# Token order, masked band products on TensorE, double weight pieces and paired inner tiles in a fused attention and gated-MLP kernel

## The chip, the cores and the metric

One core of one Trainium2 chip runs the whole program. TensorE (PE) does the products, VectorE (DVE) and ScalarE (ACT) the element work, GpSimd (POOL) some element work and some transfers, SyncE (SP) issues most transfers. The metric is the device time of one execution in microseconds, the median of several runs. The profile comes from one further execution.

## The reference, cut to what matters

```python
def attention(q, k, v):                  # 8 batches, 8 heads, 576 tokens, 64 wide
    q_d, k_d, v_d = (mean over each 4 tokens of q, k, v)         # 144 tokens
    out_d = softmax(q_d @ k_d.T / 8) @ v_d                       # "coarse"
    out_local = softmax(q @ k.T / 8 where |i - j| < 4) @ v       # "band"
    return repeat(out_d, 4) + out_local

x = attention(q, k, v) as (4608 tokens, 512)
xn = x / sqrt(mean(x * x) + 1e-6) * rms_g
out = (silu(xn @ w_gate) * (xn @ w_val)) @ w_out                 # inner width 1536
```

The weights reach the chip as 64-bit floats, 18.9 MB in all; everything else is 32-bit.

## The kernel before

**Tokens and chunks.** The 4608 tokens are worked in 18 chunks (`NCH`) of 256. A chunk is two units of 128 tokens. A unit takes tokens from both batches of a pair of batches, a stretch of four (`US`) out of each of 16 segments per batch, so all coarse output of two batches must stand before the first chunk of that pair.

**Coarse attention.** A coarse unit (class `Coarse`) is one batch and one pair of heads, 32 in all: scores on PE (L499), peaks on DVE (L508, L513), exponents on ACT (L518), turns on PE (L527), copies on ACT (L534), values on PE (L541), the share on DVE (L547, L550, L554). The result is written to DRAM and read back in token order (`load_up`), and DVE adds it (L846). The sums over four tokens come, for the first two batches, from PE products with the identity (class `OpeningSums`, L408) and DVE additions (L429), and for later ones from adding transfers that POOL issues (L362).

**Band attention.** Class `Attention` has, per chunk, four times two products of q with shifted k on DVE (L758, 128x896) and their sums (L762), a softmax over seven neighbours, products of the shares with shifted v (L812 on DVE, L805 on ACT), and the sum over neighbours: on DVE (L831), in chunks 0 and 1 on PE (L827, products with the identity). Then the root of the mean square (L863 to L886), the norm (L895), turns on PE (L907), and a split of x into a high and a low part (L911 on ACT, L915 on DVE), since products are made of two reduced-precision parts.

**The MLP.** For each of 12 inner tiles `f` PE does 12 gate and 12 value products of 128x256 (L976), ACT the tanh (L983), DVE the gate and the product (L986, L991, 128x256 each), ACT the high part (L997), DVE the low part (L1000), and PE six second products of 128x512 (L1011), two tiles later (`LAG` = 2). Gate and value of a tile share one PSUM bank. ACT evicts the result (L1018).

**The weights** are decoded in 36 pieces of 128x512: fetch the raw 64 bits (L250), scale on ACT (L254), gather the last bits on POOL (L264), join on DVE (L271), high part on ACT (L281, L283), low part (the split) on DVE (L295 with the gain, L293) or, for `w_out`, on whichever of DVE and POOL the planner picks. The scaled copy stands in a tile of its own.

```python
        def decode(n):                                   # before, shortened
            at = due[0] - 16 + 1.4 * n
            ...
            join_ = task("DVE", 0.78, join, at, [scaled, bits], uses=[raw, w])
            hi = task("ACT", 0.7, high, at, [join_, *own], uses=[w])
            if n in gained:
                whole[n] = task("DVE", 0.85, lambda: split("dve"), at, [hi], uses=[w])
```

**What sets the order.** For the opening, chunks 0 to 2 and the attention of chunk 3, class `Plan` sorts tasks like the ones above: each has an engine, a written cost, a due time, what it comes after and the buffers it takes; the planner walks a model clock and, on each engine, emits the ready task with the earliest due time. From chunk 3 on a loop emits in written order, with the attention and two coarse units for the next chunk laid between the inner tiles, and a scheduler places the instructions:

```python
        for f in range(NF):                              # before, from chunk 3
            fwd.emit(f)
            late.append((fwd, f))
            if len(late) > LAG:
                fw, g = late.pop(0)
                fw.emit_second(g)
            while todo and todo[0][0] < f + 1:
                todo.pop(0)[1]()
```

Thirty idle products on PE (L1105), fed by a copy on ACT (L1102), are planned from about 5 us with the latest due time of all.

## Time and profile before

| | us |
|---|---|
| runs | 1143.12, 1146.85, 1143.39; median 1143.39 |
| span of the profiled execution | 1142.6 |
| busy: PE, DVE, ACT, POOL | 1080.1, 963.1, 625.7, 173.0 |
| first gate product (L976) | 107.8 |
| end of chunk 0, 1, 2 (eviction L1018) | 186.3, 255.5, 316.3 |
| end of chunk 3, 4, 5 | 370.9, 444.1, 501.2 |
| end of the last chunk | 1138.3 to the last product, 1142.6 with its store |

How to read it: the time of the median run stands 0.8 us above the span, which is what lies around it. A chunk's length is the distance between the ends of two chunks. Busy shares are means over stages with different limits, so each stage is read by itself.

### The profile page before, as it was taken

To read this page: it belongs to the slowest core of one execution; us is meant where nothing else is said; L and a number is where in the kernel's file an instruction comes from. 1 tells how busy PE (TensorE), PEld (TensorE's weight loads), DVE (VectorE), ACT (ScalarE), POOL (GpSimd) and SP (SyncE) were. 2 spreads that over 40 slices of the span, in tenths; PEclk is the share of its full clock that TensorE was granted. 3 is DMA by queue.
4 is the path that set the end of the run, shared out by engine and by line. 5 is a ranking of instruction groups with operands and counts; after the bars stand their busy time and mean duration, and the time that the engine had idled before them with its cause. 6 is when DMAs were issued, how large, how long until landed. Compare 5 with 4: busy or idle time off the path is not lost.

```text
span 1142.6 us, 21949 instructions
## 1 busy us (share of the span) xinstructions
PE 1080.1 (95%) x8002; PEld 987.1 (86%) x8002; DVE 963.1 (84%) x1869; ACT 625.7 (55%) x2284; POOL 173.0 (15%) x205
## 2 busy tenths in 40 slices
PE   6883799999999999999999999999999999999998
PEld 4772688878898899999999999998999999999997
DVE  6786998788999989797989797979898989997432
ACT  1564663847383847474747474747465573838221
POOL 1654662334200010101010101000000000000000
PEclk8875999999999899999999999999999999999999
DMA  9986482446544443535253535222231313220000
GB/s 267 300 274 173 107 222 84 96 95 148 124 100 105 110 104 88 115 88 115 83 120 88 114 88 114 78 63 76 65 89 54 99 52 99 67 60 20 1 19 20
DMA packets 76813, 119.57 MB, mean 105 GB/s; under 512 B 26784, under 2 KB 36256, under 8 KB 76704
## 3 DMA queue, kind: packets, MB, share of 16 engines
q1 hardware_dynamic: 47520, 97.34, 28.8%
q0 software_dynamic: 8640, 15.93, 9.1%
q10 hardware_dynamic: 20544, 4.89, 2.0%
q8 instruction: 63, 1.03, 0.4%
q14 instruction: 46, 0.38, 0.1%
HBM read 106.33 MB, written 11.80 MB: 103 GB/s over the span
## 4 chain that ended last, share of the span: by engine, by line
PE 78%; DVE 8%; DMA 7%; ACT 2%; issue 2%; POOL 1%; SPq 0%; ACTq 0%; DVEq 0%; POOLq 0%
PE ps_h L976 48%; PE ps_o L1011 24%; PE ps_a L541 2%; PE ps_a L499 2%; DMA wg<-in_v_sum_dram 1%; DMA wg<-in_w_gate_dram 1%; DVE o_sb L271 1%; PE ps_a L907 1%; DMA qk<-in_qk_sum_dram 1%; DMA kv<-in_k_pad_dram 1%; DVE prod L812 1%; PE ps_a L527 1%; DVE prod L758 1%; ACT up_t L856 1%; ACT prod L805 1%
## 5 line engine op out<-in xcount | busy, mean ns | idle before, releaser
L1011 PE MATMUL ps_o<-wo,hs 128*128 128x512 f32 x1296 | 355.7, 399 | 5.4 <-POOL hs L1000 5.3
L976 PE MATMUL ps_h<-xh,wg 128*128 128x256 f32 x1728 | 349.1, 282 | 4.0 <-DVE wg L295 1.7
L976 PE MATMUL ps_h<-xh,wv 128*128 128x256 f32 x1728 | 341.8, 280 | 5.0 <-DVE sil L986 4.9
L976 PEld LDWEIGHTS ps_h<-xh,wg 128*128 128x128 f32 x1728 | 284.0, 190 | 13.0 <-ACT xh L911 2.2
L976 PEld LDWEIGHTS ps_h<-xh,wv 128*128 128x128 f32 x1728 | 280.5, 188 | 11.0 <-DVE sil L986 6.9
L805 ACT ACTIVATE prod<-kv,sc 128x64 f32<-128x64 f32 x1072 | 279.2, 405 | 18.1 <-DVE x_t L831 9.8
L1011 PEld LDWEIGHTS ps_o<-wo,hs 128*128 128x128 f32 x1296 | 221.2, 188 | 43.1 <-POOL hs L1000 8.4
L976 PE MATMUL ps_h<-xl,wg 128*128 128x256 f32 x864 | 243.5, 282 | 0.1
L976 PE MATMUL ps_h<-xl,wv 128*128 128x256 f32 x864 | 241.8, 280 | 0.0
L983 ACT ACTIVATE sil<-ps_h 128x256 f32<-128x256 f32 x216 | 82.4, 382 | 227.8 <-PE ps_h L976 216.0
L986 DVE SCALAR_TENSOR_TENSOR sil<-sil,ps_h 128x256 f32<-128x256 f32 x216 | 91.1, 422 | 94.9 <-ACT sil L983 83.5
L976 PEld LDWEIGHTS ps_h<-xl,wg 128*128 128x128 f32 x864 | 164.0, 190 | 6.9 <-DVE sil L986 1.3
L976 PEld LDWEIGHTS ps_h<-xl,wv 128*128 128x128 f32 x864 | 163.0, 189 | 1.6
L997 ACT ACTIVATE hs<-sil 128x256 fp32r<-128x256 f32 x216 | 89.3, 415 | 133.9 <-DVE sil L991 112.3
L758 DVE TENSOR_TENSOR prod<-q_t,kv 128x896 f32<-128x896 f32 x140 | 153.1, 1094 | 5.7 <-DMA q_t<-in_q_band_dram 5.4
L762 DVE TENSOR_REDUCE sc<-prod 128x14 f32<-128x896 f32 x144 | 155.3, 1085 | 0.4
L831 DVE TENSOR_REDUCE x_t<-prod 128x128 f32<-128x896 f32 x128 | 135.7, 1080 | 11.5 <-PE ps_a L907 4.5
L812 DVE TENSOR_TENSOR prod<-sc,kv 128x384 f32<-128x384 f32 (+2 forms) x144 | 119.6, 868 | 0.2
L1000 DVE TENSOR_TENSOR hs<-sil,hs 128x256 fp32r<-128x256 f32 x196 | 87.3, 447 | 23.3 <-ACT hs L997 23.2
L991 DVE SCALAR_TENSOR_TENSOR sil<-sil,ps_h 128x256 f32<-128x256 f32 x216 | 91.2, 422 | 6.4 <-PE ps_h L976 4.8
L362 POOL DMA_DIRECT2D qk<-in_qk_sum_dram x36 | 32.2, 894 | 319.6 <-DMA qk<-in_qk_sum_dram 275.1
L856 ACT ACTIVATE up_t<-x_t 128x128 f32<-128x128 f32 x144 | 44.2, 307 | 21.3 <-DVE x_t L846 12.7
(118 smaller groups left out, 974.7 us busy)
## 6 DMA issues: line engine op xcount, KB each, us to landing
kv<-in_k_pad_dram SPq DMA_DIRECT2D x72, 320.0 KB
kv<-in_v_pad_dram SPq DMA_DIRECT2D x72, 320.0 KB
qk<-in_qk_sum_dram POOLq DMA_DIRECT2D x36, 288.0 KB, 5.0
out_dram<-o_sb SPq DMA_DIRECT2D x36, 256.0 KB
q_t<-in_q_band_dram SPq DMA_DIRECT2D x70, 128.0 KB
vs<-in_v_sum_dram POOLq DMA_DIRECT2D x36, 144.0 KB, 3.6
...
```

Source lines behind the costliest of these rows:

```text
L758: nc.vector.tensor_tensor(out=pr, in0=bcast(q[:, s0:s0 + 2], 2, NO), in1=window(k, s0), op=ALU.mult)
L762: nc.vector.tensor_reduce(out=self.sc[:, j, par, s0:s0 + 2], in_=self.pr[i], axis=AX.X, op=ALU.add,)
L805: nc.scalar.activation(out=self.pr[i][:, o, s], in_=self.v[j, par][:, s0 + s + o], func=AF.Copy, scale=p[:, s, o:o + 1],)
L812: (nc.vector if engine == "DVE" else nc.gpsimd).tensor_tensor(out=self.pr[i][:, a:b], in0=bcast(p[:, :, a:b].rearrange("p s o -> p o s"), ...
L831: nc.vector.tensor_reduce(out=self.x[j][:, s0:s0 + 2, par], in_=pr.rearrange("p o s d -> p s d o"), axis=AX.X, op=ALU.add,)
L976: nc.tensor.matmul(out=self.p[f][:, t], lhsT=wi(f)[:, 0, k], rhs=xi[:, k], start=(n == 0), stop=(n == 3 * KT - 1),)
L983: nc.scalar.activation(out=self.sil[f], in_=self.p[f][:, 0], func=AF.Tanh, scale=0.5)
L986: nc.vector.scalar_tensor_tensor(out=self.sil[f], in0=self.sil[f], scalar=1.0, in1=self.p[f][:, 0], op0=ALU.add, op1=ALU.mult,)
L991: nc.vector.scalar_tensor_tensor(out=self.sil[f], in0=self.sil[f], scalar=0.5, in1=self.p[f][:, 1], op0=ALU.mult, op1=ALU.mult,)
L997: nc.scalar.activation(out=self.hs[f][:, 0], in_=self.sil[f], func=AF.Copy)
L1000: (nc.gpsimd if engine == "POOL" else nc.vector).tensor_tensor(out=self.hs[f][:, 1], in0=self.sil[f], in1=self.hs[f][:, 0], op=ALU.subtract,)
L1011: nc.tensor.matmul(out=self.o[j], lhsT=lhs[:, cols], rhs=rhs(f)[:, 0], start=(f == 0 and i == 0), stop=(f == NF - 1 and i == 2),)
```

## The change

1. *Tokens in order.* A unit is 32 consecutive groups of four tokens, for all heads. Batch b's four coarse units are needed only when its tokens come. Four coarse units stand in the opening, eight are planned during chunks 0 to 2, and the loop lays two per chunk from chunk 3. Loads of q, k, v and stores of the output are cut where batches and runs of nine groups end.
2. *Band attention of chunks 0 and 1 on PE* (class `Early`): scores of 128 tokens against their neighbourhood of 136, with a mask that a bf16 product adds (L1048, L1050), peaks on DVE (L1063), exponents on ACT (L1074), shares on DVE (L1101), turns (L1108, L1118) and value products (L1133) on PE. The coarse output is added by a product with a spread matrix (L1139) from SBUF, without the way through DRAM. The mask and the spread matrix are made on POOL at the start.
3. *Opening sums* for batch 0 alone, by a DVE sum over four raw slabs (L406) and, for v, additions on POOL and DVE (L415).
4. *No idle products.*
5. *Weights in double pieces*, 16 of 128x1024 and four of 128x512, decoded in place in the raw tile; the split always on DVE (L285 with the gain, L283).
6. *Inner tiles in pairs*: gate of two tiles, value of two tiles, and tanh, gate, product, high and low part once on 128x512 (L1266, L1269, L1274, L1283); second products (L1296) one pair later; gate and value in banks of their own; two buffers each for `sil` and `hs`.

```diff
-LAG = 2
-W_BUFS = 4
+LAG = 1
+W_BUFS = 2
 FIRST = 3
-EARLY = 7
-COARSE = {3: 1}
+ON_TENSOR = 2
...
-    spots = [f"first{n % 8}" for n in range(24)]
+    spots = [("first0", "first1", "first2", "first3", "second0", "second1")[n % 6] for n in range(12)]
+    spots += ["second0", "second1", "second0", "second1", "xh1", "xl1", "o_sb", "o_sb"]
...
-        join_ = task("DVE", 0.78, join, at, [scaled, bits], uses=[raw, w])
+        join_ = task("DVE", (0.78, 1.3)[m - 1], join, at, [scaled, bits], uses=[raw])
...
+        low = task("DVE", (0.75, 1.35)[m - 1], split, at, [hi], uses=[raw])
...
+    class Early:
+        def load_values(self, u):
...
+            for h in range(H):
...
+                nc.sync.dma_start(out=self.ve[u][h * EDGE:(h + 1) * EDGE, h * D:(h + 1) * D], in_=src)
+        def score(self, u, n):
...
+            nc.tensor.matmul(out=s, lhsT=one_sb, rhs=bcast(near_sb[:, FAC * (1 - lo):FAC * (1 - lo + NEAR_K)], 1, 2), start=True, stop=False)
+            for h in range(2):
+                nc.tensor.matmul(
+                    out=s[:, h].rearrange("p (n j) -> p n j", j=FAC), lhsT=q[:, h, FAC * n0:FAC * (n0 + GRP)],
+                    rhs=k[:, h, n0 - lo:n0 - lo + NEAR_K], start=False, stop=(h == 1),
+                )
...
-            n = min(COARSE.get(c, 2), len(coarse) - done)
+            n = min(2, len(coarse) - done)
...
-        for f in range(NF):
-            fwd.emit(f)
-            late.append((fwd, f))
...
+        for n in range(NF // 2):
+            for half in range(2):
+                (fwd.emit_value if half else fwd.emit_gate)(n)
+                if half:
+                    late.append((fwd, n))
+                    if len(late) > LAG:
+                        fw, g = late.pop(0)
+                        fw.emit_second(g)
+                while todo and todo[0][0] < 2 * n + half + 1:
+                    todo.pop(0)[1]()
```

**PE at the start.** In the rows below, `ps_a`, `ps_h` and `ps_o` are PSUM banks, `wo` and `wv` hold raw sums in the weights' later places, `qk` the sums, `near_sb` and `one_sb` the mask. Before:

```order
L1105 MATMUL ps_o<-hs 128x256 x21
L408 MATMUL ps_a<-wo_0_113,ident_sb 128x288 x8
L1105 MATMUL ps_o<-hs 128x256 x5
L408 MATMUL ps_h<-wo_0_138,ident_sb 128x288 x8
L499 MATMUL ps_a<-qk 72x144 x4
L408 MATMUL ps_a<-wv_0_171,ident_sb 128x288 x4
L499 MATMUL ps_h<-qk 72x144 x4
L527 MATMUL ps_a<-ident_sb,a_g 72x72 x8
```

And after the change, where `hs` is q in token order and `w_1_102` the raw k:

```order
L1048 LDWEIGHTS one_sb
L1048 MATMUL ps_h<-near_sb,one_sb 128x272
L1050 MATMUL ps_h<-w_1_102,hs 128x136 x2
L1048 LDWEIGHTS one_sb
L1048 MATMUL ps_h<-near_sb,one_sb 128x272
L1050 MATMUL ps_h<-w_1_102,hs 128x136 x2
L498 MATMUL ps_a<-qk 72x144 x4
L526 MATMUL ps_a<-ident_sb,a_g 72x72 x8
```

Sums and idle products are gone from the head of PE's row, and band scores stand there, ahead of the coarse scores.

**DVE around the first gate product.** The last thing that chunk 0's gate waits for is the low part of x, `xl`. Before:

```order
L295 SCALAR_TENSOR_TENSOR wg_0_409<-o_sb,g_sb,wg_0_408 128x4x128
L295 SCALAR_TENSOR_TENSOR wv_0_416<-o_sb,g_sb,wv_0_415 128x4x128
L915 TENSOR_TENSOR xl<-ps_a,xh 128x4x128 x2
L758 TENSOR_TENSOR prod<-q_t,kv 128x896
L762 TENSOR_REDUCE sc<-prod 128x14
L986 SCALAR_TENSOR_TENSOR sil<-sil,ps_h 128x256
```

After, where `wo_1_134` holds shares of the band attention and `w_2_216`, `w_2_281` raw pieces of weights:

```order
L1093 TENSOR_TENSOR prod<-wo_1_134,z_e 128x64
L1101 TENSOR_TENSOR wo_1_134<-wo_1_134,z_e 128x4x128 x2
L1063 TENSOR_REDUCE m_e<-ps_h 128x2
L1183 TENSOR_TENSOR xl_630<-ps_a,xh_629 128x4x128 x2
L1063 TENSOR_REDUCE m_e<-ps_h 128x2
L1067 TENSOR_SCALAR m_e<-m_e 128x4
L271 SCALAR_TENSOR_TENSOR w_2_216<-w_2_216 128x1024 x2
L271 SCALAR_TENSOR_TENSOR w_2_281<-w_2_281 128x1024
```

The low part moves from place 123 in DVE's row to place 78 (repeats counted once), and what stands ahead of it is now shares and peaks where band products, sums and splits stood.

**DVE within a later chunk.** Before:

```order
L812 TENSOR_TENSOR prod<-sc,kv 128x3x128
L986 SCALAR_TENSOR_TENSOR sil<-sil,ps_h 128x256
L885 TENSOR_TENSOR newton<-newton,rms 128x8
L812 TENSOR_TENSOR prod<-sc,kv 128x3x128
L991 SCALAR_TENSOR_TENSOR sil<-sil,ps_h 128x256
L886 SCALAR_TENSOR_TENSOR rinv<-newton,rinv 128x8
L895 TENSOR_TENSOR x_t<-x_t,rinv 128x512 x2
L1000 TENSOR_TENSOR hs<-sil,hs 128x256
```

After:

```order
L1269 SCALAR_TENSOR_TENSOR sil<-sil,ps_h 128x512
L1274 SCALAR_TENSOR_TENSOR sil<-sil,ps_h 128x512
L1283 TENSOR_TENSOR hs<-sil,hs 128x512
L874 TENSOR_REDUCE x_t<-prod 128x2x64 x2
L1269 SCALAR_TENSOR_TENSOR sil<-sil,ps_h 128x512
L934 TENSOR_TENSOR xl_8074<-ps_a,xh_8073 128x4x128 x2
L864 TENSOR_TENSOR prod<-sc,kv 128x3x128 x2
L1274 SCALAR_TENSOR_TENSOR sil<-sil,ps_h 128x512
```

Each pass of the inner tiles now covers two tiles, and band passes stand between a pair's gate and product as they stood between a tile's.

**SP ahead of the first weight.** After the change SP's row begins with the raw sums, four loads of v and 32 edge loads of 8x64, and only then come the weights:

```order
L1028 DMA wo_1_189<-in_v_pad_dram 128x8x64
L1036 DMA kv<-in_v_pad_dram 8x1x64 x8
L249 DMA w_2_216<-in_w_gate_dram 128x1024
L249 DMA w_2_216<-in_w_val_dram 128x1024
```

Before, eight loads of k and q, eight of raw sums and four of v stood there.

917 lines of the change are left out of this document (582 added, 335 removed).

## The prediction

> **What bounds the kernel now.** I read the slices of the span, then windows cut at the ends of chunks (the evictions of the second products, L1018), then the waits, the chain and the DVE groups of the opening. Columns of the windows: length, then busy time (instructions) of PE, PEld, DVE, ACT, POOL, then granted clock, DMA share, GB/s.
>
> ```profile
> PE   6883799999999999999999999999999999999998
> DVE  6786998788999989797989797979898989997432
> ...
> 0.00:107.80 107.80, 69.84 (x472) 57.60 (x472) 81.99 (x135) 49.26 (x156) 52.01 (x52) 0.78 0.88 264
> 107.80:186.30 78.50, 68.61 (x483) 62.11 (x484) 70.37 (x116) 47.37 (x118) 39.86 (x40) 0.97 0.55 138
> 186.30:255.50 69.20, 64.21 (x498) 56.44 (x497) 55.57 (x103) 38.92 (x150) 22.59 (x37) 1.00 0.41 97
> 255.50:316.30 60.80, 58.78 (x451) 53.16 (x450) 54.19 (x105) 33.16 (x129) 22.27 (x35) 1.00 0.60 132
> ...
> 370.90:444.10 73.20, 69.90 (x521) 64.32 (x522) 67.42 (x131) 49.88 (x200) 5.18 (x6) 0.95 0.38 93
> 444.10:501.20 57.10, 57.10 (x437) 52.27 (x435) 51.16 (x105) 33.39 (x130) 5.15 (x6) 1.00 0.43 102
> 842.60:893.40 50.80, 50.80 (x372) 47.71 (x371) 47.85 (x94) 28.78 (x110) 0.00 (x0) 1.00 0.27 76
> 1094.40:1142.60 48.20, 43.93 (x312) 40.64 (x311) 13.09 (x32) 9.99 (x24) 0.00 (x0) 1.00 0.06 23
> ```
>
> Two regimes. From about 444 us PE is busy for 57.10 of 57.10 us in a chunk that carries two coarse units and 50.80 of 50.80 in one that carries none, so one coarse unit costs (57.1 − 50.8)/2 = 3.15 us of PE, and nothing off PE counts there. The first 107.8 us hold no gate product; PE is busy 65% of them with sums, coarse units, turns and idle products, DVE 76%. Chunks 0 and 1 then take 78.5 and 69.2 us. What a chunk needs of PE follows from the dense stretches:
>
> ```profile
> 1131.46 2.75 PE ps_h L976 x24
> 1134.21 3.90 PE ps_o L1011 x17
> ```
>
> 114.6 ns for a gate or value product, 229 ns for a second product; 288 × 0.1146 + 72 × 0.229 = 49.5 us, some 50.5 with the turns of x (50.8 measured). So chunk 0 lost over 15 us beyond its other turns (112 of L827), and chunk 1 with some 3.6 coarse units (11 us) lost 69.2 − 50.5 − 11 = 7. What stood in the opening:
>
> ```profile
> PE ps_a L863 <- ACT up_t L856: 14.3, 1, 14.3
> PE ps_a L408 <- DMA wo<-in_qk_sum_dram: 5.0, 1, 5.0
> ...
> 8.39 15.59 DMA wg<-in_v_sum_dram
> 28.75 15.49 DMA wg<-in_w_gate_dram
> ...
> 87.32 3.94 DMA up<-o_g
> 92.28 4.22 DMA up_t<-up
> ...
> PE ps_h L976 <- DVE sil L986: 3.4, 2, 2.4
> PE ps_h L976 <- DVE wg L295: 1.7, 1, 1.7
> ```
>
> The first two are PE's waits before 107.8 (total, times, longest): coarse output written to DRAM and read back, 14.3 us at the end of the opening. The next four are from the chain (start, length). The last two are waits within chunk 0: the weights are decoded barely ahead of use.
>
> **The change, part by part.** The prices of DVE in the opening (count | busy, mean ns | idle before it):
>
> ```profile
> L762 DVE TENSOR_REDUCE sc<-prod 128x14 f32<-128x896 f32 x13 | 14.1, 1081 | 0.3
> L758 DVE TENSOR_TENSOR prod<-q_t,kv 128x896 f32<-128x896 f32 x9 | 10.2, 1132 | 5.4 <-DMA q_t<-in_q_band_dram 5.4
> L812 DVE TENSOR_TENSOR prod<-sc,kv 128x512 f32<-128x512 f32 x8 | 7.8, 980 | 0.0
> L271 DVE SCALAR_TENSOR_TENSOR o_sb<-o_sb,wg 128x512 uint32<-128x512 uint32 x8 | 5.4, 681 | 3.0 <-POOL wg L264 3.0
> L295 DVE SCALAR_TENSOR_TENSOR wg<-o_sb,g_sb,wg 128x512 fp32r<-128x512 f32 x5 | 4.5, 897 | 0.0
> L513 DVE TENSOR_SCALAR m_g<-m_g 72x4 f32<-72x4 f32 x8 | 3.8, 473 | 0.2
> L508 DVE TENSOR_REDUCE m_g<-ps_a 72x2 f32<-72x288 f32 x8 | 3.2, 443 | 0.0
> L554 DVE TENSOR_TENSOR o_g<-ps_a,z_g 72x256 f32<-72x256 f32 x4 | 1.6, 412 | 0.0
> L550 DVE RECIPROCAL z_g<-z_g 72x4 f32<-72x4 f32 x8 | 1.4, 174 | 0.3
> L429 DVE TENSOR_TENSOR vs<-vs,wg 72x512 f32<-72x512 f32 x2 | 1.4, 690 | 0.1
> ```
>
> From 512 to 896 elements per lane a pass grows from 0.69 to 1.08 us, 1.02 ns an element: I estimate 1.21 us for 1024 and 2.5 for the 2304 that one opening sum reads.
>
> *Opening, first gate product 107.8 → 70.* Leaving it: band products, sums and values of two chunks on DVE, four coarse units of eight, the idle products, PE's sums, the DRAM round trip. Ahead of chunk 0's last low part DVE's order now holds 2 opening sums (5.0), 14 peaks at about 0.43 (6.0), 4 coarse units at 2 × 0.44 + 2 × 0.47 + 0.17 + 0.41 = 2.4 (9.6), 6 double joins (7.3), 4 gained splits and 2 plain ones at 1.21 to 1.8 (8.3), 6 passes of shares (4.1), 6 copies, adds and lows (4.1) and some thirty small ones at 0.17 to 0.47 (6): 50 us where 82 stood. DVE was busy 80% from its first instruction, at about 5 us, to 107.8; the same share gives 62 us, and the sums must land first, about 7.5: 70. Lower bound 60: DVE never waits after the sums, 7.5 + 50, or the sixth weight piece paces it. SP now issues 32 small edge loads and 4 of values before the first weight, at 0.4 to 0.6 us each:
>
> ```profile
> 3.32 0.54 SPq L568 DMA_DIRECT2D kv<-in_k_pad_dram  x1
> ...
> 21.60 7.10 SPq L568 DMA_DIRECT2D kv<-in_v_pad_dram  x4
> 28.75 0.59 SPq L250 DMA_DIRECT2D wg<-in_w_gate_dram  x1
> ```
>
> 36 × 0.54 = 19 us put the first weight at about 24 us instead of 28.75; six pieces of 1.05 MB at 264 GB/s take 24 more, so the last lands near 50, and with its decoding and the rest of the row the gate opens past 60. Upper bound 82: DVE at 67% (waits on SP's loads, on POOL's thirteen steps of masks, on a slower PE). If each small load took 7.10/4 = 1.8 us, the first weight would come at 70 and nothing would be gained; those four queued behind large transfers, the small ones only behind two, so I stay near 0.54.
>
> *Chunk 0, 78.5 → 80.* It still waits for weights. From the first gate product to the last split of gate and value weights DVE's order holds 10 double joins and 4 single ones (14.9), 8 gained splits at 1.45 and 2 plain ones at 1.25, all of them now on DVE (14.1), peaks, shares and norm of chunk 1 (7.4), ten passes of the inner tiles (6.9) and six band products with their sums, for chunk 2 (13): 56 us, at chunk 0's share (70.37 of 78.5, 90%) 62.5. Behind the last split come four inner tiles' products (96 × 0.1146 = 11) and the second ones trailing (6): 80. Bounds 73 (share 1) and 90 (76%, DVE's share of the opening). PE's own work, less the 112 turns (L827), is not the limit here.
>
> *Chunks 1 and 2, 69.2 → 65 and 60.8 → 61.* PE content: 50.5 and four coarse units each, 63; DVE some 55 us at 0.9. Together the end of chunk 2 moves by −37.8 + 1.5 − 4.2 + 0.2 = −40.3.
>
> *Coarse units moved later: +9.4.* Batch order needs four at the start instead of eight, so 20 remain after chunk 2, where 17 stood: 3 × 3.15, on a full PE.
>
> *The seam in chunk 4: −3.* The window 370.90:444.10 holds 352 gate and value products, 72 second ones and about 2.5 units, 40.3 + 16.5 + 8 + 2 = 67 us of PE, so some 6.5 were lost; half, as DVE's inner-tile work falls. Bounds 0 and −6.5.
>
> *Pairs of inner tiles: 0.* PE's products stay 128x256 and 128x512 and as many. DVE's passes go from 36 to 18 per chunk at
>
> ```profile
> L986 DVE SCALAR_TENSOR_TENSOR sil<-sil,ps_h 128x256 f32<-128x256 f32 x216 | 91.1, 422 | 94.9 <-ACT sil L983 83.5
> ```
>
> 36 × 0.42 = 15.2 against 18 × 0.69 = 12.4, which is 2.8 us a chunk off an engine that has 6 free. Cover: after the values of pair p PE has the 48 products of pair p+1 (5.5 us) before it needs p's low part, and product, high, low take 0.69 + 0.59 + 0.69 = 2.0 with the eviction below for the high part; 3.5 us are left for queueing on DVE, where a band pass ahead takes 0.7 to 1.1.
>
> ```profile
> L1018 ACT COPY o_sb<-ps_o x2: 586/586/587, 185.7 to 186.4; 128x512 f32<-128x512 f32 x2
> 1138.14 1.07 ACT L1018 COPY o_sb<-ps_o 128x512 f32<-128x512 f32 x2 [2.08 <-PE ps_o L1011]
> ```
>
> *Loads and stores in pieces.* Nothing in the middle: chunk windows show DMA at 0.27 to 0.43, and SP issues up to a chunk ahead. The last store goes in some five issues instead of one, 4 × 0.54 less overlap: +0.7, bounds 0 and 2.
>
> Sum: −40.3 + 9.4 − 3 + 0.7 = −33.2 against the profiled span of 1142.6: 1109.4. The median of the runs, 1143.39, is 0.8 above that span: 1110.
>
> **A rule weighed.** The clock as rows show it:
>
> ```profile
> 28.00:57.00 29.00, 25.39 (x186) 21.02 (x185) 22.79 (x42) 16.00 (x56) 17.53 (x17) 0.88 0.98 298
> 86.00:114.00 28.00, 9.16 (x49) 7.85 (x48) 19.35 (x36) 12.18 (x33) 13.08 (x12) 0.54 0.59 174
> ```
>
> With PE 88% busy 0.88 was granted, and 0.54 in the stretch that holds the wait of 14.3 us. The change takes the idle products out and makes the opening of PE sparser. The Trainium skill, "TensorE: Matmul & The Clock Gate", section on the HAM clock gate, says that an idle PE falls to half rate after a window of some 3.4 us and needs about as long busy to return; by it the new opening could run wholly at half rate. The trace agrees in direction; no run of before is that sparse for long.
>
> **Rivals.**
> 1. *Half clock through the opening.* Ahead of the first gate product PE's order holds four coarse units (12.6) and 97 other products; at the price of the turns of before,
>
> ```profile
> L827 PE MATMUL ps_o<-prod,ident_sb 128*128 128x128 f32 x112 | 15.8, 298 | 0.1
> ```
>
> 15.8/112 = 0.14, they take 13.7: 26 us, and 26 more at half rate. Against: DVE paces the opening, and slow products hide beside its 50 us unless they chain, score to peak to turn to value. If a third of the extra (8 us) adds to the waits, the first gate product comes at 78: 1118. The page named above is what would bring this about.
> 2. *The opening gives most back.* First product at 82, chunk 0 at 80, seam as long as before: 1110 + 12 + 3 = 1125; with chunk 0 at 90, 1135. For it: chunk 0's waits on decoding, all splits now on DVE. Still faster.
> 3. *Slower: pairs starve PE in the steady part.* One pair of lag where two tiles stood. Place: the second products waiting for the low part behind band passes in DVE's fixed order. It decides when DVE's queue exceeds the 3.5 us of cover by 0.4 us on average over 14 × 6 = 84 pairs (33/84); at 0.5 us each, 42 us are lost: 1152. Against: DVE is 84 to 90% busy but its passes are 1 us long, and its load falls.
> 4. *A larger gain.* DVE never waits, first product at 60, seam gone: 1110 − 10 − 3.5 = 1097.
>
> **Numbers.** The sum as worked out 0.55, rival 1 0.12, rival 2 0.14, rival 3 0.08, rival 4 0.06, and 0.05 for an opening that gains nothing (small loads at 1.8 us), about 1143. The likeliest case's own range is 1102 to 1118; from 1097 to 1135 leaves out rival 3, the last case and tails of the others, some 2 in 10. A change of 0.3% (3.4 us) is about what a measurement of this kernel can tell from none: faster 0.87, same 0.04, slower 0.09.
>
> **What would show it.** First gate product (L1259) at 60 to 82, DVE about 50 us busy ahead of it; the last split of gate and value weights some 62 us later, PE waiting on it; evictions of chunks 0, 1, 2 near 150, 215 and 276; chunks of 57 with two coarse units and 51 without; nothing but small waits on the low part. Wrong if PE waits for the low part in every pair, if the first weight is issued past 35 us, or if chunk 0 exceeds 90 us.

## The result, and the profile after

| | before | after |
|---|---|---|
| runs, us | 1143.12, 1143.39, 1146.85, 1146.97 | 1128.91, 1130.23, 1137.31, 1138.12 |
| median | 1145.12 | 1133.77 |
| profiled span | 1142.6 | 1135.5 |
| first gate product | 107.8 | 89.4 |
| end of chunk 0, 1, 2 | 187.0, 256.1, 317.1 | 184.4, 253.7, 317.6 |
| end of chunk 3, 4, 5 | 373.3, 446.6, 503.7 | 376.7, 434.3, 491.3 |
| end of the last chunk | 1139.2 | 1130.1 |

The ratio is 0.9887, with an interval of 0.9839 to 0.9936: 11.4 us faster. The forecast was 33 us. The direction held; the size was a third. The profiled execution of after is one of its two longer ones (1137.31), so the two spans differ by 7.1 us where the medians differ by 11.4. Of the experiments below, one execution of 2104.2 us, of the kernel with values in bf16 and the edges of two units late, fell in a slow state and is left out of median and ratio. Ends of chunks here and below are ends of the evictions; those of before in the prediction are their starts or some 1.4 us ahead of them.

The slices of the span of the changed kernel, PE, DVE and PE's granted clock:

```profile
PE   4699969989999999999999999999999999999997
DVE  5365987869997979797979797979797989887321
PEclk9999989989999999999999999999999999999999
```

PE reaches the nines in the third slice now, at about 57 us, where before the third read 8 and the fourth 3. That looks like the gain that was forecast. The windows cut at the same places show that it is not. They have the columns of the prediction's windows: length, busy time (instructions) of PE, PEld, DVE, ACT, POOL, granted clock, DMA share, GB/s. The first five are the opening, its last 29 us apart, and chunks 0 to 2; then chunk 5 and a chunk without coarse units.

```profile
0.00:89.40 89.40, 61.67 (x273) 45.06 (x274) 48.22 (x91) 44.93 (x122) 32.48 (x40) 1.00 0.64 213
60.00:89.40 29.40, 28.03 (x102) 19.12 (x103) 20.59 (x45) 21.20 (x55) 12.21 (x7) 1.00 0.65 228
89.40:184.40 95.00, 83.21 (x521) 71.78 (x520) 74.74 (x110) 51.34 (x116) 26.35 (x26) 0.95 0.50 130
184.40:253.70 69.30, 63.31 (x468) 54.60 (x467) 49.56 (x86) 36.18 (x137) 25.47 (x37) 0.93 0.53 120
253.70:317.60 63.90, 63.90 (x500) 59.77 (x499) 60.07 (x95) 42.52 (x164) 12.42 (x23) 1.00 0.46 107
...
434.30:491.30 57.00, 57.00 (x440) 52.95 (x439) 49.86 (x88) 31.94 (x118) 5.23 (x6) 1.00 0.42 101
886.20:937.00 50.80, 50.80 (x374) 47.81 (x373) 47.07 (x76) 27.69 (x98) 0.00 (x0) 1.00 0.26 76
```

DVE did its 48.22 us ahead of the first gate product, but PE was busy for 61.67 of those 89.40 us, and for 28.03 of the last 29.40. Chunk 0 then took 95.0 us instead of 79.2. So at the end of chunk 2 nothing had been gained in this profile: 317.6 against 317.1. The gain came behind it. Windows over chunks 3 and 4 of before and of after:

```profile
317.10:446.60 129.50, 126.17 (x951) 116.57 (x951) 119.17 (x233) 85.25 (x344) 10.39 (x12) 0.97 0.41 98
```
```profile
317.60:434.30 116.70, 116.70 (x904) 108.11 (x903) 101.73 (x180) 66.08 (x244) 13.81 (x16) 1.00 0.48 109
```

12.8 us less, with PE busy throughout. Part of that had been done ahead. Counts of the first products by the end of chunk 2, of before (four rows, 876) and of after (two, 937):

```profile
L976 PE MATMUL ps_h<-xh,wg x297: 276/278/583, 107.8 to 317.0; 128*128 128x256 f32 x149
L976 PE MATMUL ps_h<-xh,wv x288: 276/276/388, 112.8 to 308.9; 128*128 128x256 f32 x144
L976 PE MATMUL ps_h<-xl,wg x147: 276/277/580, 108.6 to 316.8; 128*128 128x256 f32 x147
L976 PE MATMUL ps_h<-xl,wv x144: 276/276/287, 112.9 to 308.8; 128*128 128x256 f32 x144
```
```profile
L1259 PE MATMUL ps_h<-xh,w x625: 276/276/582, 89.4 to 317.5; 128*128 128x256 f32 x157
L1259 PE MATMUL ps_h<-xl,w x312: 276/276/420, 89.8 to 317.3; 128*128 128x256 f32 x156
```

Three chunks need 864. Twelve were ahead before, 73 are now, and at 0.1146 us the 61 more are 7.0 us of chunks 3 and 4. Against them stand three coarse units fewer, 12 done where 15 were, 9.4 us at 3.15. So by PE's work, too, the opening and chunks 0 to 2 gained nothing in this profile; all of its gain lies behind them. From the end of chunk 2 to the last eviction the times are 822.1 before and 812.5 after: +9.4 for three coarse units more, −7.0 for the products ahead, −7.8 in the seam, chunks 3 and 4, where the planned part meets the loop (649 first products, 4 units and 144 second products make some 120 us of the 129.5, so 9.5 were lost there; 578 and 5 units make 115 of the 116.7, so 1.7), and −4.2 over the thirteen chunks that follow, which no run here splits further.

**Why the opening took 89 us.** SP's issues of the changed kernel (start, length): the first and the last group of the 32 edge loads and the first weight. Then the 32 loads one by one (shortest, median and longest in ns), and waits of SP (total, times, longest), the last of them at 96 us:

```profile
2.35 9.99 SPq L1036 DMA_DIRECT2D kv<-in_v_pad_dram  x8
...
29.48 5.24 SPq L1036 DMA_DIRECT2D kv<-in_v_pad_dram  x8
34.77 0.40 SPq L249 DMA_DIRECT2D w<-in_w_gate_dram  x1
```
```profile
L1036 SPq DMA_DIRECT2D kv<-in_v_pad_dram x32: 272/611/3632, 2.4 to 34.1; - x32
...
SPq L1036 <- DMA w<-in_qk_sum_dram: 3.3, 2, 2.8
SPq L1036 <- POOL sil L1379: 3.2, 1, 3.2
SPq L1036 <- DMA w<-in_v_sum_dram: 3.0, 2, 2.5
...
SPq L593 <- PE ps_a L1133: 22.6, 2, 21.2
```

A row that merges eight loads holds the waits between them too. One load took 0.61 us to issue in the median; 30 of the 32 took 0.54 on average, the other two 3.63 and 1.57. Between loads SP stood 7.5 us in all, until the raw sums and the first loads of v had landed. So the first weight was issued at 34.8, not at 24. ACT stood at its scaling until weights had landed, with copies for PE queued behind it, and PE waited for ACT:

```profile
ACT w L254 <- DMA w<-in_w_val_dram: 10.2, 1, 10.2
PE ps_a L1108 <- ACT a_g L605: 10.0, 1, 10.0
```

PE's groups up to the first gate product (busy, mean ns of one), and a DVE group:

```profile
L1050 PE MATMUL ps_h<-w,hs 64*128 64x136 f32 x56 | 18.0, 456 | 2.4 <-ACT hs L402 2.4
L1133 PE MATMUL ps_o<-w,prod 128*128 128x64 f32 x32 | 7.3, 424 | 0.0
L1139 PE MATMUL ps_o<-xl,wo 72*128 72x512 f32 x4 | 3.9, 1088 | 0.0
```
```profile
L406 DVE TENSOR_REDUCE qk<-w 128x576 f32<-128x2304 f32 x2 | 8.4, 4190 | 6.5 <-DMA w<-in_qk_sum_dram 6.5
```

Together PE's work that is not coarse took some 42 us ahead of the first gate product, where the prediction had 13.7. One reason is the count: a group counts records, and by the code an fp32 product leaves two, a turn or a bf16 product one. The 112 records that gave the prediction's 0.14 us are 56 products; the 97 products here leave 145 records, some 20 us at 0.14. The other reason is what a record takes, for which PE's rate is one cause. PE's timeline, the 16 records of a unit's eight value products, once before and once behind the change of rate:

```profile
72.38 3.67 PE L1133 MATMUL ps_o<-w,prod 128*128 128x64 f32 x16
117.86 2.00 PE L1133 MATMUL ps_a<-wo,prod 128*128 128x64 f32 x16
```

The same work took 3.67 us and later 2.00. The granted clock reads 1.00 in both windows that hold the opening's end. But this trace has no entry of the clock ahead of 107.5 us, and what has none counts as full in the column. Equal instructions set side by side showed the low rate; in x_block below, whose clock has entries from 33 us on, the column shows it too.

**Why chunk 0 took 95 us.** Its last weights are decoded in places (pieces of SBUF used twice) that band attention of chunk 1 holds until its last product with the spread matrix. The chain (start, length):

```profile
121.31 0.88 PE ps_a L1139 x2
122.20 0.59 ACT x_t L605
122.79 1.03 ACT wo L278
123.85 1.24 DVE wo L283
125.14 0.33 SPq L249
125.52 6.86 DMA wo<-in_w_val_dram
...
145.35 6.86 DMA wo<-in_w_val_dram
...
156.74 1.29 DVE w L285
158.07 3.14 PE ps_h L1259 x13
```

Two rounds of place, transfer, decoding: 36 us from the last product of chunk 1's band attention to the last gained split. Some 5 us of them are band passes of chunk 2 that stand in DVE's row there. In every run of the changed kernel and its variants below, q_on1 apart, the last split ends 35 to 42 us behind that product.

### The profile page after: what moved, and what is told of

Its sections match the earlier page's. It is cut to its first block, busy times and chain, and to the rows that moved or that the text cites. A ratio compares the mean times of both kernels' runs of the same rounds, so it can differ in the third digit from the quotient of the medians.

```text
span 1135.5 us, 21446 instructions
## 1 busy us (share of the span) xinstructions
PE 1083.9 (95%) x7878; PEld 987.3 (87%) x7878; DVE 900.8 (79%) x1519; ACT 597.8 (53%) x2033; POOL 142.2 (13%) x178
## 3 DMA queue, kind: packets, MB, share of 16 engines
q8 instruction: 62, 1.02, 0.4%
## 4 chain that ended last, share of the span: by engine, by line
PE 88%; DMA 5%; DVE 2%; ACT 2%; SPq 1%; issue 1%; POOL 0%; ACTq 0%; DVEq 0%; POOLq 0%
PE ps_h L1259 50%; PE ps_o L1296 25%; PE ps_a L540 3%; PE ps_a L498 2%; PE ps_a L526 2%; PE ps_a L926 1%; DMA wo<-in_w_val_dram 1%; PE ps_o L1133 1%; SPq L1036 1%; PE ps_h L1050 1%; DMA w<-in_v_pad_dram 1%; DMA w<-in_v_sum_dram 1%; PE ps_a L1133 1%; DMA q_t<-in_q_band_dram 1%; PE ps_a L1108 0%
## 5 line engine op out<-in xcount | busy, mean ns | idle before, releaser
L1259 PE MATMUL ps_h<-xh,w 128*128 128x256 f32 x3456 | 635.5, 281 | 10.7 <-ACT w L278 6.4
L1259 PEld LDWEIGHTS ps_h<-xh,w 128*128 128x128 f32 x3456 | 540.3, 189 | 22.7 <-ACT w L278 6.8
L1259 PE MATMUL ps_h<-xl,w 128*128 128x256 f32 x1728 | 483.5, 280 | 0.0
L1296 PE MATMUL ps_o<-wo,hs 128*128 128x512 f32 x1296 | 333.5, 399 | 1.7 <-POOL hs L1283 1.6
L1259 PEld LDWEIGHTS ps_h<-xl,w 128*128 128x128 f32 x1728 | 327.2, 189 | 6.5 <-issue 1.7
L1296 PEld LDWEIGHTS ps_o<-wo,hs 128*128 128x128 f32 x1296 | 233.4, 189 | 46.4 <-POOL hs L1283 2.7
L1266 ACT ACTIVATE sil<-ps_h 128x512 f32<-128x512 f32 x108 | 64.5, 597 | 168.3 <-PE ps_h L1259 159.7
L1280 ACT ACTIVATE hs<-sil 128x512 fp32r<-128x512 f32 x108 | 68.2, 631 | 155.0 <-DVE sil L1274 134.2
L1269 DVE SCALAR_TENSOR_TENSOR sil<-sil,ps_h 128x512 f32<-128x512 f32 x108 | 73.5, 681 | 50.1 <-ACT sil L1266 49.8
L864 DVE TENSOR_TENSOR prod<-sc,kv 128x384 f32<-128x384 f32 (+1 forms) x128 | 103.6, 865 | 0.2
L1274 DVE SCALAR_TENSOR_TENSOR sil<-sil,ps_h 128x512 f32<-128x512 f32 x108 | 74.4, 690 | 30.5 <-PE ps_h L1259 30.3
L1283 DVE TENSOR_TENSOR hs<-sil,hs 128x512 fp32r<-128x512 f32 x100 | 68.7, 687 | 18.9 <-ACT hs L1280 18.7
L517 ACT ACTIVATE a_g<-ps_a,m_g 72x144 f32<-72x144 f32 x128 | 46.4, 370 | 15.1 <-DVE m_e L1067 8.3
```

Source lines behind the costliest of these rows:

```text
L864: (nc.vector if engine == "DVE" else nc.gpsimd).tensor_tensor(out=self.pr[i][:, a:b], in0=bcast(p[:, :, a:b].rearrange("p s o -> p o s"), ...
L1259: nc.tensor.matmul(out=p[n][:, i], lhsT=wi[:, k], rhs=xi[:, k], start=(m == 0), stop=(m == 3 * KT - 1),)
L1269: nc.vector.scalar_tensor_tensor(out=self.sil[n], in0=self.sil[n], scalar=1.0, in1=self.g[n], op0=ALU.add, op1=ALU.mult,)
L1274: nc.vector.scalar_tensor_tensor(out=self.sil[n], in0=self.sil[n], scalar=0.5, in1=self.v[n], op0=ALU.mult, op1=ALU.mult,)
L1283: (nc.gpsimd if engine == "POOL" else nc.vector).tensor_tensor(out=self.hs[n][:, 1], in0=self.sil[n], in1=self.hs[n][:, 0], op=ALU.subtract,)
L1296: nc.tensor.matmul(out=self.o[j], lhsT=lhs[:, cols], rhs=rhs, start=(f == 0 and m == 0), stop=(f == NF - 1 and m == 2),)
```

## The experiments

All were timed against the kernel before, whose median was 1145.1 to 1148.1 us beside them, so ratios compare better across rows than times do. Times are medians; T1 is the first gate product, then the end of chunk 0 and the last gained split, each from the profile of that kernel.

| kernel | us | ratio, interval | T1 | chunk 0 ends | last split |
|---|---|---|---|---|---|
| after | 1133.77 | 0.9887 [0.9839, 0.9936] | 89.4 | 184.4 | 158.0 |
| the same, second | 1131.96 | 0.9879 [0.9835, 0.9923] | 89.3 | 178.5 | 151.5 |
| the same, third | 1132.13 | 0.9874 [0.9845, 0.9902] | 89.1 | 178.2 | 150.7 |
| 140 idle products | 1136.88 | 0.9881 [0.984, 0.9921] | 106.2 | 182.5 | 156.4 |
| one edge load a unit | 1121.37 | 0.9777 [0.9742, 0.9812] | 81.5 | 170.8 | 143.7 |
| both of these | 1127.47 | 0.9823 [0.9779, 0.9867] | 94.1 | 170.8 | 144.8 |
| one head's values | 1128.09 | 0.9812 [0.9779, 0.9845] | 83.3 | 170.3 | 143.9 |
| one edge load, one head's values | 1121.15 | 0.9752 [0.9724, 0.9781] | 75.5 | 166.9 | 140.3 |
| loads planned behind weights | 1139.32 | 0.9923 [0.9897, 0.995] | 90.1 | 175.2 | 152.5 |
| edges behind first weights | 1141.24 | 0.9933 [0.9901, 0.9965] | 89.1 | 184.0 | 153.0 |
| values in bf16 | 1131.69 | 0.9853 [0.9824, 0.9882] | 82.1 | 176.5 | 146.7 |
| the same, edges of two units late | 1132.22 | 0.9844 [0.9798, 0.9891] | 93.1 | 182.6 | 156.0 |
| 40 idle products in a block | 1135.24 | 0.988 [0.9857, 0.9903] | 86.6 | 181.9 | 155.7 |
| that block, values in bf16 | 1133.08 | 0.9861 [0.983, 0.9892] | 82.4 | 177.6 | 146.8 |
| chunk 1's band work on DVE | 1153.73 | 1.0056 [1.0041, 1.0071] | 81.9 | 171.6 | 151.4 |
| before, no idle products | 1146.77 | 1.0005 [0.9989, 1.002] | 107.1 | | |
| before, pairs | 1142.97 | 0.9967 [0.995, 0.9983] | 103.1 | 190.9 | |
| edges in two loads a unit | 1128.14 | 0.9845 [0.9815, 0.9874] | 85.5 | 176.5 | 146.9 |
| that, values in bf16 | 1126.96 | 0.9831 [0.9803, 0.9858] | 84.0 | 168.8 | 139.5 |

**PE's rate.** Kernel a_same is the changed kernel again; c_idle140 puts 140 bf16 products of the identity on PE wherever nothing else is ready.

```diff
+    for i in range(140):
+        task("PE", 0.15, idle_product, 1e6 + i, [], allocs=[idle] if i == 0 else [], uses=[idle], not_before=3 + 0.3 * i)
```

> The changed kernel again, beside the others on one chip. Expected 1128 to 1138 us, first gate product near 89, end of chunk 0 near 184, last split of gate and value weights near 158. Every theory says the same here; it is the base for the other three runs.

> The changed kernel with 140 idle bf16 products of 128x256 on PE, planned with the latest due time, so that they stand where the planner saw PE idle up to the second band unit's coarse addition. Theory 1, half rate: PE runs the opening at half rate (213 ns for a gate product, 0.24 for a score product) until about 108 us because nothing there raises it; with idle products the score products of the opening fall to about 0.12 us and the 16 value products of a unit from 3.7 to 2.0. PE was 93% busy from 41 us on, so the first gate product comes 10 to 18 us earlier (72 to 79), the loads queued on SP behind a buffer that PE frees (21 us) come earlier, the last split falls to 140 to 148, and the whole is 8 to 16 us below the changed kernel. Theory 2, small loads: the opening is paced by SP's 32 edge loads, first weight at 34.8 us; then PE's rate is hidden, the first gate product moves by under 4 us and the whole by under 4. Theory 3, decode: the first gate product moves but the last split stays within 4 us of 158, and the whole within 4.

The second run of the changed kernel was an experiment by itself: T1 was the same, 89.3, but PE's rate rose earlier. The two edge products ahead of a unit's values, in after and then in a_same:

```profile
92.25 2.07 PE L1133 MATMUL ps_a<-kv,prod 64*128 64x512 f32 x2
```
```profile
92.07 1.12 PE L1133 MATMUL ps_a<-kv,prod 64*128 64x512 f32 x2
```

At the same place and time one took 2.07 us and the other 1.12. In a_same SP came free at 111.7 instead of 118.0, and chunk 0 ended 5.9 us earlier, chunk 2 6.8. So the rate is worth about 6 us of the time, and it need not be the same from run to run. The idle products lifted it in four stretches, the longest from 61.7 to 85.6 us. Rows of c_idle140 in it, and one of a_same at the high rate:

```profile
77.86 1.19 PE L1050 MATMUL ps_h<-w,hs 64*128 64x136 f32 x4
78.98 2.03 PE L1422 MATMUL ps_o<-ident_sb 128*128 128x256 bf16 x17
```
```profile
95.16 1.18 PE L1050 MATMUL ps_h<-w,hs 64*128 64x136 f32 x4
```

Seventeen idle products in 2.03 us are 119 ns each, near the high rate, and the four score records (L1050) beside them took 1.19 us where they took 1.29 at the low rate; they hardly follow it. The idle products held PE for 24.3 us. T1 went to 106.2, but not by them alone: the plan of this kernel also puts 41 records of chunk 1's band attention ahead of the first gate product (314 records besides the idle ones, where 273 stood), so T1 does not price them. The whole gained nothing.

**The small loads.** d_oneedge keeps the load of one head's edge rows of each unit and leaves seven out; e_both adds the idle products.

```diff
             for h in range(H):
...
-                nc.sync.dma_start(out=self.ve[u][...], in_=src)
+                if h == 0:
+                    nc.sync.dma_start(out=self.ve[u][...], in_=src)
```

> The changed kernel with one edge load per unit instead of eight: the edge neighbours of heads 1 to 7 in chunks 0 and 1 are left out (zeros stand there), all products stay. SP's small loads before the first weight fall from 32 to 4. Theory 2, small loads: first weight issued at 15 to 18 us instead of 34.8, ACT's and PE's wait of 10 us at 31 to 41 goes, first gate product 12 to 18 us earlier, whole 8 to 15 below the changed kernel. Theory 1, half rate: PE stays at half rate and its 60 us of opening work at that rate is the bound; only the wait of 10 us goes, first gate product 6 to 10 earlier, and the whole 3 to 8 below. Theory 3, decode: weights 17 us earlier all along, last split 10 to 17 earlier, whole 8 to 15 below.

> Both edits: one edge load per unit (edge neighbours of heads 1 to 7 in chunks 0 and 1 left out) and 140 idle products. If half rate and small loads are separate costs on the same path, the gains add: first gate product at 60 to 66, last split 125 to 138, whole 18 to 28 below the changed kernel, about 1105 to 1115, near what the sum had forecast. If one hides the other, the whole is within 4 us of the better of the two single edits.

```profile
18.52 0.40 SPq L249 DMA_DIRECT2D w<-in_w_gate_dram  x1
```

The first weight came 16.3 us earlier, 0.58 for each of the 28 loads left out, T1 7.8, and chunk 0 ended 13.6 us earlier than in after, 7.7 earlier than in a_same. Against the second run of the changed kernel (1131.96) the whole gained 10.6 us, so the small loads are dear. With the idle products as well, in the same order of PE's row as in c_idle140, 6 us of it were lost.

**The value products.** h_onevalue leaves out the value products of seven of eight heads; z_oneedge_onevalue leaves out both.

```diff
-            for h in range(H):
+            for h in range(1):
                 cols = slice(h * D, (h + 1) * D)
                 todo.append((
```

> The changed kernel with the value products of heads 1 to 7 of chunks 0 and 1 left out on PE (the turns, shares, edge and coarse products stay): 14 records of 0.213 us less per unit, 3.0 us per unit, 12 us of PE in all. Theory A, PE's opening row: the last six weight pieces go into places that hold shares of chunk 1, so they wait for the end of chunk 1's band work on PE (115 to 121 us), and the last split follows 37 us behind it; then that end comes 6 to 12 us earlier, the last split too (to 142 to 150), and the whole is 6 to 12 us below the changed kernel (1120 to 1126). Theory B, decoding by DVE and ACT: PE's products are hidden, the last split stays within 3 us of 151 to 158 and the whole within 3 us.

> One edge load per unit and one head's value products in chunks 0 and 1 (edges and values of heads 1 to 7 left out). Alone they moved the first gate product from 89.3 to 81.5 and 83.3, and the last gained split from 151.5 to 143.7 and 143.9. If they add: first gate product at 74 to 77, last spread product near 98, last gained split at 134 to 138, whole 14 to 20 below the changed kernel (1112 to 1119): then loads and PE's products explain some 15 of the 19 us that the first gate product came late. If DVE or ACT stands behind both, the first gate product stays above 79 and the whole above 1120.

T1 fell by 6.1 without the value products, and by 13.9 without both (7.8 + 6.1). So both stand on the path to T1 one behind the other, and PE's own work is on it. 5.5 us between 75.5 and the forecast 70 stay. The whole gained nothing that the intervals tell over the edge loads alone, 0.9752 against 0.9777; chunk 2 grew to 69.8.

**The order of loads.** By the last of its waits above, SP stood 21 us at a load of v (L593) for PE's values, ahead of the fetches for the last weights. g_sp_order plans that load and its like behind the fetch of the last double piece; k_edges_late plans v and edge loads of units 1 to 3 behind the first weights; w_bf16_edges23 does so for units 2 and 3 and takes values in bf16; o_bf16 takes values in bf16 alone.

```diff
+            for t in atts[ON_TENSOR].loads + atts[ON_TENSOR + 1].all_loads:
+                t.after.append(got)                                          # g
-                v_got = task("SP", 0.9, lambda u=u: self.load_values(u), -90 + 12 * u, [clear], ...)
+                v_got = task("SP", 0.9, lambda u=u: self.load_values(u), 8 + u if u else -90, [clear], ...)   # k
```

> The changed kernel with the band loads of chunk 2 (third and fourth of k and q, all of v) and of chunk 3 planned behind the fetch of the last double piece of weights, so that SP does not stand 16 to 21 us at a v load that waits for a buffer which PE frees. Theory C, SP's queue: the fetches behind that load come 15 us earlier, last split near 140, whole 8 to 15 below the changed kernel. Theory A: the next fetch in SP's row goes to a place that holds the coarse output, which PE frees with its last spread product some 3 us later, so SP stands there instead; last split within 4 us of the changed kernel's 151 to 158, less what the k and q loads between the pieces cost (3 to 8 us), whole 0 to 6 below.

> The changed kernel with the v and edge loads of units 1 to 3 planned behind the first weight pieces (nothing left out): the first weight is issued at about 15 us instead of 34.8. By the run with one edge load per unit the wait of 10 us at 31 to 41 us goes and the first gate product comes at 80 to 84, the whole 6 to 11 us below the changed kernel. Rival: the edges of unit 1 now come late and its value products hold up PE, which works in order; then the first gate product stays at 87 to 92 and the whole within 3 us.

> The changed kernel with the value products of chunks 0 and 1 in bf16 (turned shares written as bf16, v rounded in place by POOL): one record instead of two per product and a fourth of the cost of a fp32 product, some 0.11 us instead of 0.43 per head at the low rate, 2.6 us less per unit and 10 in all. Theory A: as in the run with one value product, last split at 142 to 150, whole 6 to 10 below the changed kernel. If bf16 products also raise PE's rate where fp32 ones did not, the turns and spreads of chunk 1 take half, and the whole is 10 to 16 below. Theory B: within 3 us.

> Two edits on the changed kernel: value products of chunks 0 and 1 in bf16, and the v and edge loads of units 2 and 3 (not unit 1) behind the first weight pieces. The first weight is issued near 24 us instead of 34.8. Units 0 and 1 have their edges in time, so the wait for the late first weight shrinks by some 5 us and bf16 takes 2.6 us per unit: first gate product at 76 to 80, last spread product at 96 to 104, last gained split 40 behind it, whole 6 to 14 below the changed kernel (1119 to 1126). If units 2 and 3 now wait for their edges, the first gate product still moves but the last spread stays near 106 and the whole within 3 us of the run with bf16 alone.

g moved neither T1 nor the split (152.5), and the whole came no lower than the changed kernel's: behind SP's wait stands another, for the place that the last spread product frees at 117.4. k brought the first weight to 13 us and T1 not at all (89.1): ACT now stood 11.0 us, with a store of coarse output next in its row, until an edge load had landed, and PE stood 10.1 us for ACT's exponents behind it. o_bf16 moved T1 by 7.3 and chunk 0 by 2.0 against a_same, and the whole by nothing that the intervals can tell. w gave T1 93.1: its plan put a unit of chunk 1 ahead of the first gate product, 276 records of PE where o_bf16 had 257, so its T1 does not tell what the loads' order is worth.

**Idle products in one block** at PE's wait of 10 us, 40 of them (x_block), and with values in bf16 (x_block_bf16).

```diff
         def turn_edge(self, u):
+            if u == 0:
+                ...
+                for _ in range(40):
+                    nc.tensor.matmul(out=t[:, :C], lhsT=some[:, :P], rhs=some, start=True, stop=True)
```

> The changed kernel with 40 idle bf16 products of 128x256 in one block ahead of unit 0's turn of edge shares, where PE stood 10 us waiting (31 to 41 us); nothing else changed. Theory 1, low rate: PE leaves the block at the full rate, unit 0's value products take 3.0 instead of 5.6 us and its turns half; if the rate held to the first gate product that would come 10 to 15 us earlier (75 to 80) and the whole 8 to 14 below; in the run with 140 idle products the rate fell again within 10 us under score products, so I expect 3 to 6 us of it: first gate product at 83 to 87, whole 2 to 6 below the changed kernel. If the rate does not matter because DVE and ACT hand over late, the first gate product stays within 2 us of 89.

> The same block of idle products, with the value products of chunks 0 and 1 in bf16. bf16 alone gave a first gate product at 82 and 1130 to 1133 us. If rate and number of products add, the first gate product comes at 77 to 80 and the whole 3 to 6 below bf16 alone (1125 to 1129); if bf16 already took away what the rate cost on this path, within 2 us of bf16 alone.

PE's timeline of x_block (in brackets the idle time ahead):

```profile
30.80 5.59 PE L1120 MATMUL ps_o<-ident_sb 128*128 128x256 bf16 x40
41.29 1.12 PE L1108 MATMUL ps_a<-ident_sb,w 128*128 128x128 f32 x4 [4.79 <-ACT a_g L605]
...
71.50 2.00 PE L1138 MATMUL ps_o<-w,prod 128*128 128x64 f32 x16
```

The block itself reached 109 ns, but 4.79 us idle behind it, and the four turns took 1.12 us, as they do in the changed kernel without the block. At 71.5 a unit's values were at the full rate, 2.00 us; its first unit's, at 48, had taken 3.67. T1 gained 2.8 us and the whole nothing. With values in bf16 the block moved T1 no further, 82.4 against 82.1. Windows of x_block:

```profile
60.00:70.00 10.00, 9.88 (x44) 7.12 (x45) 8.27 (x15) 7.56 (x23) 2.69 (x1) 0.50 0.76 234
70.00:78.00 8.00, 8.00 (x38) 5.04 (x36) 5.71 (x9) 7.49 (x18) 5.00 (x5) 0.93 0.80 319
```

The column shows the low rate and its rise at 70.5 us, behind the same rows of PE that left it low in the changed kernel.

**Chunk 1 on DVE.** q_on1 leaves only chunk 0's band attention on PE (`ON_TENSOR = 1`).

> The changed kernel with the band attention of chunk 0 alone on PE; chunk 1's runs on DVE and ACT as that of chunk 2 does (8 times a product, a sum, a value product and a value sum of about 1.1, 1.1, 0.9 and 1.1 us on DVE, 33 us in all, less 8 of shares and peaks). Theory A, places: no weight piece then waits for chunk 1's work on PE, the last spread product is unit 1's, before 80 us, and the last gained split comes at 110 to 130 us instead of 151 to 158; PE is rid of some 25 us of products at the low rate. What DVE gains in work (25 us) delays that in part. Whole 5 to 18 below the changed kernel. Theory B, DVE: DVE is the bound of the opening, so 25 us more on it make the end of chunk 1 15 to 25 later: whole 10 to 25 above the changed kernel.

Windows of q_on1, chunks 0 and 1:

```profile
81.90:171.60 89.70, 63.00 (x370) 55.00 (x370) 79.74 (x98) 48.78 (x117) 36.49 (x31) 0.83 0.54 139
171.60:264.20 92.60, 76.94 (x550) 68.50 (x551) 69.05 (x122) 47.31 (x179) 24.96 (x39) 0.85 0.46 104
```

The last spread product came at 72.5, 49.7 us sooner, and the last split still at 151.4: here DVE, busy for 79.74 of 89.70 us, paces the decoding. Chunk 1 took 92.6 instead of 69.3, and the kernel lost to the one before. The band work of chunk 1 on PE is worth about 20 us.

**Parts of the change alone, on the kernel before.** r_before_noidle takes its 30 idle products out; s_before_pairs gives it the pairs of inner tiles, with `LAG = 1` and `W_BUFS = 2`, and nothing else.

> The kernel before without its 30 idle products, nothing else changed. If the idle products are what raised PE's rate there at about 13 us (the identity sums then take 0.24 us each instead of 0.48), PE runs the opening at the low rate, identity turns of band products take 0.21 instead of 0.11 us, and the first gate product comes 5 to 20 us later than 107.8, the whole 4 to 15 above the kernel before. If DVE paces that opening whatever PE does, the first gate product moves by under 3 us and the whole by under 3.

> The kernel before with the paired inner tiles alone (gate of two tiles, value of two tiles, element passes on 128x512, one pair of lag); for room the decoding keeps two scaled copies instead of four. If pairs cost and bring nothing where PE is full, chunks from the sixth on take 57 with two coarse units and 50.8 without, within 0.3. If pairs ended the loss at the start of chunk 4 (PE idle some 3.5 us there in the kernel before, and products at the low rate behind it), the time from the end of chunk 2 to the end falls by 4 to 8 us; if that was the order of the coarse units or of the tokens, by under 2. The opening may be 0 to 10 slower for the two copies that are missing; the whole then 5 below to 8 above the kernel before.

Without the idle products nothing changed, 1.0005. With pairs, chunks 3 and 4 took 118.8 us instead of 129.5, and from the end of chunk 2 to the last eviction 812.9 instead of 822.1, with 30 more products done ahead (3.4 us): some 6 us are the pairs' own. The opening and chunks 0 to 2 gave part of it back (323.5 at the end of chunk 2 against 317.1), and 4 us stayed.

**A version without the small loads.** v_oneload computes everything: each unit's edge rows come compactly, in two loads of 32 rows, and POOL lays them out with a product with a block mask in place of clearing the tile. a_again is the changed kernel on the same chip.

```diff
-                nc.sync.dma_start(out=self.ve[u][h * EDGE:(h + 1) * EDGE, h * D:(h + 1) * D], in_=src)     # x8
+                nc.sync.dma_start(out=self.vc[u][i * H * FAC:(i + 1) * H * FAC], in_=src)                  # x2
-            nc.gpsimd.memset(self.ve[u], 0.0)
+            nc.gpsimd.tensor_tensor(out=self.ve[u]..., in0=bcast(self.vc[u], 1, H), in1=bcast(block_sb[:, :H], 2, D), op=ALU.mult)
```

> The changed kernel with the whole computation, but each unit's edge rows come in two loads of 32 rows instead of eight of 8, and POOL spreads them over the heads' columns (a product with a block mask) where it cleared the tile. Theory A (the issue time of the 32 loads delays the first weight, and that delays everything to the end of chunk 0): the first weight issued near 20 us instead of 34.8, the first gate product at 82 to 84 instead of 89.4, the end of chunk 0 at 171 to 175, and 1122 to 1127 us, ratio to the kernel before 0.978 to 0.983. Rival B (the gain that one edge load per unit showed came from the work left out, fewer bytes and fewer waits, and here POOL's four products of 64x512, behind the loads and ahead of its additions of v, stand in the way of the coarse values): the first gate product stays at 88 or later, and the time is that of the changed kernel, 0.988.

> The same loads, and the value products of the first two chunks in bf16 (shares and v rounded by the copies that write them and by one POOL copy per unit). If both savings add, as leaving out edge loads and value products did (13.8 us to the first gate product): first gate product at 75 to 77, last gained split at 139 to 143, 1119 to 1125 us, 0.975 to 0.982. If the place for the last weight pieces is what is left, as with those two together: the first gate product moves but the time stays that of the kernel with the loads alone, 1122 to 1127.

> The changed kernel once more, on the chip of the two others, so that they are set against it and not only against the kernel before: 1130 to 1138 us, 0.988, with the first gate product at 89.3 and the end of chunk 0 at 178 or at 184, by whether PE's rate rises near 92 or near 108 us.

SP's first weight, and counts of the first products by the end of chunk 2 (301.7), in v_oneload:

```profile
21.26 0.44 SPq L250 DMA_DIRECT2D w<-in_w_gate_dram  x1
```
```profile
L1265 PE MATMUL ps_h<-xh,w x598: 276/276/581, 85.5 to 301.6; 128*128 128x256 f32 x200
L1265 PE MATMUL ps_h<-xl,w x299: 276/276/415, 85.9 to 301.5; 128*128 128x256 f32 x150
```

The first weight came at 21.3 and T1 at 85.5, 3.7 us earlier than in a_again: half of what the kernel with loads left out had shown, so theory A held in direction. Whether the other half was work left out there, or the extra work of POOL and DVE here, no run tells apart. The end of chunk 2 came 11.8 us earlier than in a_again (301.7 against 313.5), but with 897 products done instead of 937, and 40 × 0.1146 = 4.6 us go back. 2.2 more go in the chunks behind chunk 4, which took 698.0 us against 695.8, for a cause that stays open. 4.4 remain at the last eviction; the spans differ by 4.5 and the medians by 4.0. With values in bf16 the median is 1.2 lower still, inside the intervals; T1 came at 84.0 and not at the 75 to 77 expected, with a unit of chunk 1 ahead of it as in w. By their medians these two are the fastest kernels here that leave nothing out, 0.9845 and 0.9831 of the kernel before against 0.9874 for the changed one; the intervals overlap, so the step over the changed kernel is likely and not shown.

## Why the prediction was right in direction and wrong in size

Against the forecast span the profiled one is 26.1 us longer: +19.4 to T1, +22.2 from T1 to the end of chunk 2, −16.8 behind it, +1.3 in the tail.

*First gate product 70, measured 89.4.* DVE's work ahead of it was right, 48.2 for 50. Three steps failed.
- "36 × 0.54 = 19 us put the first weight at about 24 us". The price held, 0.54 for 30 of the 32; that nothing else stops SP did not. It stood 7.5 us between loads for the landing of the raw sums and of v, two loads took 3.63 and 1.57, and the first weight came 10.8 us late. The 7.10 us for four loads that the prediction weighed as 1.8 each held waits in the same way (0.54, 3.45, 1.04 and 0.54). Taking most of the loads away gave 7.8 us of T1, making them few but whole 3.7.
- "They take 13.7", the 97 products other than coarse at the turns' 0.14. They took some 42. The 0.14 is a record's price and the products leave 145 records; a score record took 0.32 us (18.0/56), one of 512 columns 0.98 (3.9/4); and nearly all ran at the low rate. This is the term that was mis-sized most.
- "DVE paces the opening, and slow products hide beside its 50 us." With some 42 us of such work, beside four coarse units, PE was the longer chain: taking out value products alone moved T1 by 6.1 us, and 28 of their records at 0.21 are 6.0. Rival 1 had the mechanism, half rate, and gave it 8 us and a chance of 0.12. The two opening sums were 4.19 us each and not 2.5, on top. Of the 19.4 us, loads and value products explain 13.9; 5.5 stay open.

The share of 80% for DVE rested on a stretch in which DVE was the longest queue. It fell to about 60% when PE became that.

*Chunk 0 80, measured 95.0; chunks 1 and 2 65 and 61, measured 69.3 and 63.9.* From T1 to the last split 62.5 us were forecast; 62.2 passed in a_same and 68.6 in after, where PE's rate rose 16 us later. But the 62.5 came from DVE's queue, and what set the time was the places: last spread product, two rounds of transfer and decoding. In q_on1, where that place was free early, DVE's queue did take 69.5. Two chains of nearly one length stood there, and the forecast had one. From the last split to the end of chunk 0, 26.4 us passed for 17; 6.6 of these are 58 products of chunk 1, done ahead. The 61 for chunk 2 lay below the prediction's own 63 us of PE for it; PE was busy for all of the 63.9. "PE's own work … is not the limit here" failed as in the opening.

*Coarse units moved later, +9.4.* Right in count: 20 units lay behind chunk 2 (5 in chunks 3 and 4, 15 behind them), where before 17 did (4 and 13). The price is near too, (57.0 − 50.8)/2 = 3.1.

*The seam, −3.* Right in place, too small: −7.8. By the same count s_before_pairs lost 3.6 us there, where the kernel before lost 9.5, so the pairs alone do 5.9 of it.

*Pairs of inner tiles, 0.* Right where PE is full: chunks of 57.0 and 50.8. No wait of PE on anything stands in the list between 317.6 us and 1086; rival 3 did not come.

*Last store, +0.7.* Measured +2.0, at the edge of its bounds. The end behind the last eviction grew from 3.4 to 5.4; nine issues took 3.40 us where two took 0.82.

```profile
1129.40 3.40 SPq L1313 DMA_DIRECT2D out_dram<-o_sb  x9
```

*Rivals and signs.* In number rival 2 (the opening gives most back, up to 1135, chance 0.14) came nearest, but its first product at 82 and its chunk 0 of 90 were still too early, and its seam, unchanged, was not so. Of the signs of being wrong one came, chunk 0 above 90 us; the first weight, at 34.8, stood just short of another.

*The rule weighed.* In x_block the low rate came back in 4.79 us of idle PE. The Trainium skill, "TensorE: Matmul & The Clock Gate", Part 1: The HAM clock gate, says that about 3.4 us idle bring the half rate, and about 3.4 us of sustained work the full one. The first half agrees with that row, but it is not the only way: the clock of x_block fell again at 77.3 us and that of c_idle140 at 85.6, with PE at work up to then. The second half does not hold here: of 29.40 us PE was busy 28.03, and the value records still took 3.67 us where they later took 2.00; in x_block the same rows did bring the rise, at 70.5 us. The Trainium skill, same page, Part 4: PE-mode transpose, says that transposes don't count as busy for the gate in the same way; the turns are such, some 8.7 of these 28 us, and no run here told them apart from the small fp32 products around them. What lifts the rate in the opening stays open.
